# A SwiGLU feed-forward kernel: the first loads all issued from SyncE's queue instead of from SyncE and ScalarE

## The chip, the core and the metric

The kernel runs on one core of a Trainium2 chip. A core has five engines that run side by side and meet only at semaphores: TensorE (PE, matrix products; PEld is its weight load, which overlaps the products), VectorE (DVE), ScalarE (ACT), GpSimd (POOL) and SyncE (SP). A transfer (DMA) is issued by an instruction on SP's or ACT's own stream of instructions; the profile names these issues SPq and ACTq, and the packets that follow from them move on queue q1 (issued by SP) and queue q10 (issued by ACT). Both queues are served by the same 16 DMA engines.

The metric is device time in microseconds (us) of one execution. Before the change it is 163.66 us, the median of three runs from 163.46 to 163.86.

## The reference

The kernel computes a gated feed-forward layer: x is 2048 rows of 640, the gate and up weights are 640 x 1536, the down weight is 1536 x 640, all bfloat16.

```python
def reference(x, w_gate, w_up, w_down):
    g = _silu(x @ w_gate)
    u = x @ w_up
    return (g * u) @ w_down
```

## The kernel before, in words

The rows of x are taken in four blocks of 512 (NSB = 4, S_BLK = 512). For each block the hidden dimension of 1536 is walked in 12 column groups of 128 (KF = 12). For a group, five matmuls over the 640 input columns (KD = 5) make `pg` (gate) and five make `pu` (up); `proj` at L193 writes both, so line L195 carries them. ScalarE takes silu of `pg` (L212), VectorE multiplies it with `pu` (L213) and leaves the result in `aT`. After the 12 groups the block is projected down (L270 for the last 128 columns, L299 for the first 512) and stored. VectorE also works out the last four rows of x with dot products (L148) beside all this, and that has no part in the change.

The matmuls need x turned, with its columns on the partitions (`xT`), while it lies in memory row by row. For the first 256 rows TensorE turns it: `load_x` brings two chunks of 128 rows into `x_sb` (L86), `transpose_chunk` turns each with five matmuls against an identity (L186), and ScalarE and VectorE copy the results into `xT` (L191). All other rows are turned by a crossbar load: `turn_x` (L108 to L110) issues a DMA that transposes on its way. The first crossbar load brings rows 256 to 511 (called here *the first turn*).

The weights come in chunks of column groups, W_CHUNKS = (0,2), (2,4), (4,8), (8,12). The first chunk, 256 columns of gate and of up, is wanted first; it was cut at K_CUT = 2 into a part with input groups 0 and 1 and a part with input groups 2 to 4.

What this document calls the head of the kernel are the first nine or so microseconds:

- SP issues x chunk 0 (L112), gate groups 0:2, up groups 2:5, and the first turn (L121). ACT issues x chunk 1 (L113), gate groups 2:5, up groups 0:2. The loop at L115 to L120 crosses them over in this way. Only then does ACT run a one-column activation (L122), whose use is that the table for silu is loaded early.
- SP goes on with the second weight chunk (gate, up), the third, the fourth, the down weight (L126), the turn of the next 512 rows, and so on. All of these are issued from SP (L123 to L141), so each stands in SP's stream behind the ones before it.
- TensorE follows the order written in `head()` (L217 to L251), fixed by `keep_order`: 18 small matmuls on a tile of ones that produce nothing used (L177, `warm`), the five transposes of x chunk 0, the five of chunk 1, two more of the small ones, then 14 matmuls on gate for the first 256 rows (L237), 10 on up for the same rows (L195), and then, for rows 256 to 511, five on gate and five on up for each of two column groups. The last kind needs the first turn. After it the loop over the groups of 512 columns begins.

Completion semaphores of the DMAs are taken in rotation from a set of eight; an issue waits for the completion of the DMA that used the same semaphore before, eight DMAs earlier in the program.

Of the kernel before, what the change touches and what calls it, by code (L numbers as in the profile page):

```python
# [10 lines left out]
def _body(  # L11
# [8 lines left out]
    nc = tc.nc  # L20
# [12 lines left out]
    KD = D // P  # L33
# [10 lines left out]
    K_CUT = 2  # L44
    ROW_J = 0
    W_CHUNKS = [(0, 2), (2, 4), (4, 8), (8, 12)]
# [12 lines left out]
    wg_sb = consts.tile([P, KD, F], bf16)  # L59
    wu_sb = consts.tile([P, KD, F], bf16)  # L60
# [14 lines left out]
    wg_v = w_gate.rearrange("(kd p) f -> p kd f", p=P)  # L75
    wu_v = w_up.rearrange("(kd p) f -> p kd f", p=P)
    wd_v = w_down.rearrange("(kf p) d -> p kf d", p=P)

    def wslice(a, b):
        return slice(a * P, b * P)  # L80

    def load_w(eng, dst, src, a, b):
        eng.dma_start(out=dst[:, :, wslice(a, b)], in_=src[:, :, wslice(a, b)])

    def load_x(eng, c0, c1):
        eng.dma_start(out=x_sb[:, c0:c1, :], in_=x_v[:, c0:c1, :])  # L86
# [21 lines left out]
    def turn_x(c0, c1):  # L108
        s_sl = slice(c0 * P, c1 * P)
        nc.sync.dma_start_transpose(out=xT[:, :, s_sl], in_=xt_v[s_sl])  # L110

    load_x(nc.sync, 0, 1)  # L112
    load_x(nc.scalar, 1, 2)  # L113
    f_sl = wslice(*W_CHUNKS[0])
    for dst, src, first, second in (  # L115
        (wg_sb, wg_v, nc.sync, nc.scalar),
        (wu_sb, wu_v, nc.scalar, nc.sync),
    ):
        for eng, k_sl in ((first, slice(0, K_CUT)), (second, slice(K_CUT, KD))):
            eng.dma_start(out=dst[:, k_sl, f_sl], in_=src[:, k_sl, f_sl])  # L120
    turn_x(PE_X, SUB)  # L121
    nc.scalar.activation(silu_first[:], ones[:, 0:1], ACT.Silu)  # L122
    for a, b in W_CHUNKS[1:]:  # L123
# [6 lines left out]
    def turn_w(dst, src):  # L130
# [7 lines left out]
        out=x_row[:],  # L138
        in_=x2[S - T : S, :].rearrange("t d -> (t d)").partition_broadcast(P),
# [114 lines left out]
    for sb in range(NSB):  # L254
# [27 lines left out]
        for q in range(P // Q):  # L282
            nc.scalar.dma_start(
                out=out2[
                    sb * S_BLK : sb * S_BLK + n_t, DA + q * Q : DA + (q + 1) * Q
                ].rearrange("(i r) c -> r i c", r=Q),
                in_=ot_q[q * Q : (q + 1) * Q, :].rearrange("r (i c) -> r i c", c=Q),
            )

        for j in range(SUB):  # L290
# [5 lines left out]
            for c0, c1, tag in cols:  # L296
# [10 lines left out]
                if c1 < D:  # L307
                    nc.scalar.copy(ot[:], po[:])  # L308
                    eng = nc.sync
                else:  # L310
                    nc.vector.tensor_copy(out=ot[:], in_=po[:])  # L311
                    eng = nc.scalar
# [81 lines left out]
def kernel(tc, *args):  # L394
    _body(tc, *args)
    tc.close()
    tc.compile()
    _trim(tc.nc)
# [30 lines left out]
```

## Time and profile before

| what | value |
|---|---|
| runs, median (lowest to highest) | 163.66 us (163.46 to 163.86) |
| span of the profiled execution, first to last instruction | 162.2 us |
| around the span (median less span) | 1.46 us |
| VectorE busy | 110.9 us, 68% of the span |
| ScalarE busy | 42.7 us, 26% |
| TensorE weight loads busy | 77.9 us, 48% |
| DMA moved | 15.86 MB, 98 GB/s over the span |
| share of the 16 DMA engines, queue of SP and queue of ACT | 37.7% and 4.1% |

The page is of one execution. The span runs from the first to the last instruction of the core; the runs' times hold about 1.5 us more than it. A busy TensorE in the profile is a TensorE with matmuls in its pipe; how fast they follow each other has to be read from their starts. For DMAs there are three views: when the issuing engine spent time on the issue, how long after the start of the issue the transfer had landed (its semaphore complete), and how many packets of which size moved in a stretch of time on each queue. The loads of weights move in packets of 512 B (first and second chunk) or 1024 B, those of x chunks in packets of 1280 B, and crossbar loads in packets under 512 B, so they can be told apart.

### The profile page before, as it was taken

The numbers are of one execution on the slowest core, as the hardware profiler recorded it, in microseconds if no ns is written. First come the engines' busy times: TensorE is split into PE (matmuls) and PEld (weight loads), VectorE is DVE, ScalarE is ACT, GpSimd is POOL, SyncE is SP. The second block draws the span as 40 slices with busy tenths as digits, with TensorE's granted clock in tenths as the row PEclk, the third lists the DMA queues.
The fourth block names the chain that finished last, engine by engine and source line by source line (L and its number), as shares of the span: only waits on it lengthen the run. The fifth ranks groups of instructions, "written<-read, shape, count | busy, mean of one in ns | idle before, by whom it ended". The sixth has DMA issues, their size and how long they took to land.

```text
span 162.2 us, 2118 instructions
## 1 busy us (share of the span) xinstructions
PE 159.8 (99%) x798; PEld 77.9 (48%) x798; DVE 110.9 (68%) x249; ACT 42.7 (26%) x74; POOL 0.6 (0%) x6
## 2 busy tenths in 40 slices
PE   9999999999999999999999999999999999999995
PEld 8854444444444444444444444444444444445454
DVE  2042233599469999979919999979964999993000
ACT  5132222112222222221222322221214222222121
POOL 1000000000000000000000000000000000000000
PEclk9999999999999999999999999999999999999999
DMA  7999999994179992003110000000320000000312
GB/s 208 258 339 348 362 218 249 219 234 94 34 185 178 224 195 61 4 0 34 65 65 0 0 4 2 0 0 2 63 69 32 0 0 0 0 0 4 50 39 73
DMA packets 42441, 15.86 MB, mean 98 GB/s; under 512 B 33216, under 2 KB 42304, under 8 KB 42432
## 3 DMA queue, kind: packets, MB, share of 16 engines
q1 hardware_dynamic: 33536, 14.72, 37.7%
q10 hardware_dynamic: 8896, 1.02, 4.1%
q8 instruction: 6, 0.10, 0.2%
q14 instruction: 3, 0.02, 0.1%
HBM read 6.88 MB, written 2.62 MB: 59 GB/s over the span
## 4 chain that ended last, share of the span: by engine, by line
PE 99%; DVE 0%; issue 0%
PE pu L195 32%; PE pg L195 31%; PE po_a L299 26%; PE po_t L270 6%; PE pw L177 1%; PE pg L237 1%; PE pt L186 1%; DVE ot_b L311 0%; DVE ones L106 0%
## 5 line engine op out<-in xcount | busy, mean ns | idle before, releaser
L195 PE MATMUL pu<-xT,wu_sb 128*128 128x512 bf16 (+2 forms) x250 | 59.8, 370 | 0.0
L195 PE MATMUL pg<-xT,wg_sb 128*128 128x512 bf16 (+2 forms) x240 | 58.5, 374 | 0.0
L213 DVE TENSOR_TENSOR aT<-sg,pu 128x512 bf16<-128x512 f32 (+1 forms) x48 | 32.8, 683 | 32.8 <-PE pu L195 28.1
L212 ACT ACTIVATE sg<-pg 128x512 f32<-128x512 f32 (+1 forms) x48 | 28.6, 596 | 71.2 <-PE pg L195 68.1
L299 PE MATMUL po_a<-wd_sb,aT 128*128 128x512 bf16 (+2 forms) x216 | 42.8, 358 | 0.0
L148 DVE SCALAR_TENSOR_TENSOR prod<-wgT,x_row 128x640 f32<-128x640 bf16 x48 | 39.4, 821 | 1.1
L148 DVE SCALAR_TENSOR_TENSOR prod<-wuT,x_row 128x640 f32<-128x640 bf16 x48 | 39.4, 822 | 1.0
L195 PEld LDWEIGHTS <-wu_sb 128*128 128x128 bf16 x250 | 24.4, 98 | 27.6 <-DMA wu_sb<-in_w_up_dram 0.3
L195 PEld LDWEIGHTS <-wg_sb 128*128 128x128 bf16 x240 | 23.5, 98 | 26.9
L299 PEld LDWEIGHTS <-aT 128*128 128x128 bf16 x216 | 20.7, 98 | 21.6
L308 ACT CAST ot<-po_a 128x512 bf16<-128x512 f32 (+1 forms) x17 | 9.5, 560 | 32.0 <-PE po_a L299 20.8
L270 PE MATMUL po_t<-aT,wd_sb 128*128 128x512 bf16 (+1 forms) x48 | 10.4, 366 | 0.0
L270 PEld LDWEIGHTS <-wd_sb 128*128 128x128 bf16 x48 | 4.7, 98 | 5.1
L311 DVE CAST ot_b<-po_a 128x128 bf16<-128x128 f32 x1 | 0.3, 291 | 9.9 <-PE po_a L299 9.9
L279 ACT CAST ot_t<-po_t 128x512 bf16<-128x512 f32 (+1 forms) x4 | 2.2, 558 | 11.6 <-PE po_t L270 11.6
L148 DVE DVE_READ_ACCUMULATOR prod<-wuT,x_row 128x1 f32 x48 | 3.9, 82 | 0.0
L148 DVE DVE_READ_ACCUMULATOR prod<-wgT,x_row 128x1 f32 x48 | 3.9, 82 | 0.0
L281 DVE STREAM_TRANSPOSE ot_q<-ot_t 128x512 bf16<-128x512 bf16 (+1 forms) x4 | 2.7, 678 | 1.7 <-ACT ot_t L279 1.7
L177 PE MATMUL pw<-ones 128*128 128x128 bf16 x20 | 2.5, 313 | 0.4 <-DVE ones L106 0.4
L191 DVE COPY xT<-pt 128x384 bf16<-128x384 bf16 x2 | 0.7, 358 | 2.9 <-PE pt L186 2.9
L237 PE MATMUL pg<-xT,wg_sb 128*128 128x128 bf16 (+1 forms) x14 | 2.3, 360 | 0.0
L177 PEld LDWEIGHTS <-ones 128*128 128x128 bf16 x20 | 2.1, 148 | 0.4 <-DVE ones L106 0.4
(15 smaller groups left out, 7.6 us busy)
## 6 DMA issues: line engine op xcount, KB each, us to landing
wd_sb<-in_w_down_dram SPq DMA_DIRECT2D x1, 1920.0 KB, 14.5
out_dram<-ot SPq DMA_DIRECT2D x15, 128.0 KB, 1.7
wg_sb<-in_w_gate_dram SPq DMA_DIRECT2D x2, 640.0 KB, 7.7
wu_sb<-in_w_up_dram SPq DMA_DIRECT2D x2, 640.0 KB, 8.7
x_row<-in_x_dram SPq DMA_DIRECT2D x1, 640.0 KB, 4.7
out_dram<-ot_q ACTq DMA_DIRECT2D x12, 32.0 KB, 1.9
wg_sb<-in_w_gate_dram SPq DMA_DIRECT2D x1, 320.0 KB, 4.9
wu_sb<-in_w_up_dram SPq DMA_DIRECT2D x1, 320.0 KB, 5.4
```

What stands on the lines that cost most here:

```text
L148: nc.vector.scalar_tensor_tensor(out=prod[:], in0=wT[:, fc, :], scalar=1.0, in1=x_row[:, t, :], op0=ALU.mult, op1=ALU.mult, accum_out=acc[ ...
L177: nc.tensor.matmul(pw[:, 0:P], lhsT=ones[:], rhs=ones[:], start=True, stop=True)
L186: nc.tensor.transpose(out=pt[:, kd - k0, :], in_=x_sb[:, c, kd * P : (kd + 1) * P], identity=ident[:],)
L195: nc.tensor.matmul(ps[:, c0:c1], lhsT=w_sb[:, kd, fc * P : (fc + 1) * P], rhs=xT[:, kd, sb * S_BLK + c0 : sb * S_BLK + c1], start=(kd == 0 ...
L212: nc.scalar.activation(sg[:, 0:n_s], pg[:, 0:n_s], ACT.Silu)
L213: nc.vector.tensor_tensor(out=aT[:, fc, s0 : s0 + n_s], in0=sg[:, 0:n_s], in1=pu[:, 0:n_s], op=ALU.mult)
L237: nc.tensor.matmul(pg[:, c0:c1], lhsT=wg_sb[:, kd, wslice(fc, fc + 1)], rhs=xT[:, kd, c0:c1], start=(kd == 0 and c0 == 0), stop=(kd == KD ...
L270: nc.tensor.matmul(po_t[:], lhsT=wd_sb[:, kf, DA:D], rhs=aT[:, kf, sb * S_BLK : sb * S_BLK + n_t], start=(kf == 0), stop=(kf == KF - 1),)
L279: nc.scalar.copy(ot_t[:], po_t[:])
L281: nc.vector.transpose(out=ot_q[:], in_=ot_t[:])
L299: nc.tensor.matmul(po[:], lhsT=aT[:, kf, s0 : s0 + P], rhs=wd_sb[:, kf, c0:c1], start=(kf == 0), stop=(kf == KF - 1),)
L308: nc.scalar.copy(ot[:], po[:])
```

## The change

All loads of the head are issued by SP, one after another: x chunk 0, x chunk 1, gate groups 0:2, gate groups 2:5, the whole of up's first chunk in one DMA, then the first turn. ScalarE issues none of them; its first work is the activation with its table load. Everything after that stands in the same order as before. One DMA fewer is issued in all, since up's first chunk is no longer cut.

```diff
     load_x(nc.sync, 0, 1)
-    load_x(nc.scalar, 1, 2)
+    load_x(nc.sync, 1, 2)
     f_sl = wslice(*W_CHUNKS[0])
-    for dst, src, first, second in (
-        (wg_sb, wg_v, nc.sync, nc.scalar),
-        (wu_sb, wu_v, nc.scalar, nc.sync),
-    ):
-        for eng, k_sl in ((first, slice(0, K_CUT)), (second, slice(K_CUT, KD))):
-            eng.dma_start(out=dst[:, k_sl, f_sl], in_=src[:, k_sl, f_sl])
+    for k_sl in (slice(0, K_CUT), slice(K_CUT, KD)):
+        nc.sync.dma_start(out=wg_sb[:, k_sl, f_sl], in_=wg_v[:, k_sl, f_sl])
+    load_w(nc.sync, wu_sb, wu_v, *W_CHUNKS[0])
     turn_x(PE_X, SUB)
     nc.scalar.activation(silu_first[:], ones[:, 0:1], ACT.Silu)
     for a, b in W_CHUNKS[1:]:
```

## The prediction

> **What bounds the kernel now.** I read the page first: busy times and the chain that ended last.
>
> ```profile
> span 162.2 us, 2118 instructions
> ...
> PE 159.8 (99%) x798; PEld 77.9 (48%) x798; DVE 110.9 (68%) x249; ACT 42.7 (26%) x74; POOL 0.6 (0%) x6
> ...
> PE 99%; DVE 0%; issue 0%
> ```
>
> TensorE is the whole chain. A load costs time only where it makes TensorE wait, and each such wait in the head moves the end by as much. So I read the timeline of the head next (start, duration, engine; the bracket is an idle time and what ended it).
>
> ```profile
> 0.00 0.40 SPq L86 DMA_DIRECT2D x_sb<-in_x_dram  x1
> 0.12 0.41 ACTq L86 DMA_DIRECT2D x_sb<-in_x_dram  x1
> ...
> 0.57 0.45 ACTq L120 DMA_DIRECT2D wg_sb<-in_w_gate_dram  x1
> ...
> 1.04 0.51 ACTq L120 DMA_DIRECT2D wu_sb<-in_w_up_dram  x1
> 1.43 1.63 SPq L110 DMA_TRANSPOSE xT<-in_x_dram  x1
> ...
> 3.61 2.34 PE L237 MATMUL pg<-xT,wg_sb 128*128 128x128 bf16 x14
> ...
> 5.80 1.01 PEld L195 LDWEIGHTS <-wu_sb 128*128 128x128 bf16 x10 [0.32 <-DMA wu_sb<-in_w_up_dram]
> 5.80 1.29 PE L195 MATMUL pu<-xT,wu_sb 128*128 128x256 bf16 x10
> ...
> 6.92 0.71 PE L195 MATMUL pg<-xT,wg_sb 128*128 128x256 bf16 x5
> ```
>
> Issue plus time to landing gives when each load is there; the start of its first reader gives when it is wanted.
>
> - x chunk 1: 0.12 + 2.7 = 2.82; its weight loads come after the five transposes of chunk 0, which start at 2.29 and follow every 0.11: 2.83. No slack.
> - gate 0:2: 0.46 + 2.8 = 3.26, wanted 3.51. Gate 2:5: 0.57 + 3.6 = 4.17, wanted 4.47.
> - up 2:5: 0.92 + 4.7 = 5.62. Up 0:2: 1.04 + 4.7 = 5.74. The last gate matmul starts at 5.53 and its five predecessors of that size, from 4.47, came every 0.212, so up is wanted at 5.74 and used at 5.80: a wait of 0.06.
> - first turn: 1.43 + 5.4 = 6.83. The ten up matmuls from 5.80 follow every 0.11, as those after them do, and end at 6.90; gate goes on at 6.92. Slack 0.07.
> - second chunk: gate 3.11 + 4.9 = 8.01, wanted 9.00; up 3.73 + 5.4 = 9.13, wanted 9.97. Later loads have more: the third gate chunk 5.32 + 5.6 = 10.9, wanted near 13.2.
>
> The same 256-column matmul takes 0.212 up to 5.7 and 0.11 from 5.8. TensorE runs at half pace for its first 5.4 us of work, so in this stretch it is late itself, and loads have only to keep up with that.
>
> **The change: what SP now does.** SP takes over x chunk 1 (0.41) and gate 2:5 (0.45); up as one DMA has the size and shape of the second chunk's gate load (0.57) in place of 0.47; each added issue brings a gap of some 0.05. New issue times: x chunk 1 0.46, gate 0:2 0.92, gate 2:5 1.38, up 1.88, first turn 2.50, second chunk 4.18 and 4.80. So x chunk 1 is issued 0.34 later, the first turn and all behind it 1.07 later.
>
> *Upper bound*: every landing moves with its issue. Then x chunk 1 lands at 3.16, gate 2:5 at 4.98, up at 6.58, the first turn at 7.90. From up TensorE would be at the turn's reader at 6.58 + 1.10 = 7.68, so the turn binds: 7.90 - 6.88 = 1.02 us. The second chunk, at 9.08 and 10.2, is wanted at 10.0 and 11.0 by then. Price 1.02.
>
> *Lower bound*: landings are set by the bytes ahead, not by the issue. The packet views speak for this one. Packets and the share of each queue, 0.9 to 1.1, 1.3 to 1.5, 2.5 to 2.75 and 5 to 5.25 us:
>
> ```profile
> DMA packets 8, 0.01 MB, mean 51 GB/s; under 512 B 0, under 2 KB 8, under 8 KB 8
> ```
>
> ```profile
> DMA packets 31, 0.04 MB, mean 192 GB/s; under 512 B 1, under 2 KB 31, under 8 KB 31
> ...
> q10 hardware_dynamic: 1, 0.00, 1.7%
> ```
>
> ```profile
> DMA packets 130, 0.06 MB, mean 248 GB/s; under 512 B 9, under 2 KB 130, under 8 KB 130
> ```
>
> ```profile
> DMA packets 42, 0.01 MB, mean 46 GB/s; under 512 B 37, under 2 KB 42, under 8 KB 42
> ```
>
> A first packet moves about 1.0 us after its issue (SP's x chunk, issued at 0.00). ACT's x chunk, issued at 0.12, has its first packet only in 1.3 to 1.5, behind SP's chunk: the second queue buys no place. Issued at 0.46 it could begin at 1.46, the same time within 0.06. For the others I add up the bytes: 255 kB have moved by 2.0, 416 by 2.5, 543 by 3.0, 684 by 3.5, 826 by 4.0, 984 by 4.5. In the new order gate 2:5 begins after 459 kB, near 2.67 (its issue allows 2.38); up after 656 kB, near 3.4 (allows 2.88); the turn after 984 kB, at 4.5 (allows 3.50, and 5.1 for its last part by the 1.63 us its issue takes). Each is ready before its turn in the stream. SP's queue alone also keeps the rate: 291 to 294 GB/s at 7.0 to 8.5 us in 512 B packets, against 248 to 316 for the two queues between 2.5 and 4.5. I therefore take landings as unchanged, with 0.06 for x chunk 1 (bounds 0 and 0.33).
>
> *The turn.* Its packets (under 512 B) begin at 4.0, 122 by 4.5 and 367 more by 5.0, nearly stop from 5.0 to 5.25, and run at 566 in the half microsecond from 5.5. In the stop only a few last 512 B packets move. The same is seen at 22.3 to 22.9, where 6 and 7 packets of the down weight move per 0.3 us and the next turn starts only after them. I read it so: a crossbar load advances when the slowest DMA engine is through with the loads ahead. Those loads are the same bytes after the change, so the turn lands at 6.83, up to 0.15 later if fewer of its packets went ahead of the stop.
>
> *Up.* ACT's queue moved its last 512 B packets at 5.0 to 5.25 (2) and 31 at 4.5 to 4.75, yet up 0:2 had landed only at 5.74; the two x chunks landed 1.2 and 1.4 us after their first packets. With up wholly ahead of the turn on one queue I expect it by 5.6, so the wait of 0.06 goes. The Trainium skill, "DMA: Bandwidth & Descriptors", section on queues, rings and completion order, says the semaphore write of a DMA lands only after every earlier write of that DMA engine, across its queues. By that rule up 0:2's completion on ACT's queue was held behind turn packets of SP's queue, and the change would free it: a gain, but no more than the 0.06 that TensorE waited; the trace agrees in the lateness, and cannot show the order itself.
>
> *ScalarE.* Its table load begins at 1.58 and lasts 1.28, to 2.86; without three issues it begins near 0.2 and is done by 1.5. Its first needed work, the copy at 2.99, waits for TensorE's transposes. Gain nothing; loss nothing. POOL issues no load. SP's later issues: up's second chunk was already held at its issue (1.55 us instead of 0.57, until 5.28), which takes up the later start at 4.80, so the queue refills at the same time.
>
> **Sum.** x chunk 1 +0.06, so gate ends at 5.80; up is there; ten matmuls at 0.11 end at 6.90; the turn, between 6.83 and 6.98, is used between 6.92 and 7.00 instead of 6.92: 0 to 0.08, taken as +0.05. Span 162.2 + 0.05, with the 1.46 us around it 163.7 us. All after 7 us keeps its slack.
>
> **Rivals.**
>
> *The delay is carried* (slower). SP becomes the bound: descriptors of one issuer come too slowly, and x chunk 1, gate and the turn move with their issues. For it: the slack of x chunk 1 and of the turn is 0.01 and 0.07, and between 2.5 and 2.75 the rate sags to 248 GB/s, as if descriptors were short even with two issuers. Against it: the sums above, with 0.3 to 1.0 us to spare for all but x chunk 1. It decides from a turn landing 0.4 late; price up to 1.02, 164.7; half carried 164.2.
>
> *The pace of TensorE rises later* (slower). Half pace lasted from 0.40 to 5.80. If a gap for x chunk 1 at 2.83 made that stretch start again, full pace would come 5.4 later, at 8.2; 2.4 us at half pace lose 1.2: 164.9. Against it: the gap would be 0.06 to 0.33 us. The Trainium skill, "TensorE: Matmul & The Clock Gate", part 1, says full clock comes after a busy window of about 3.4 us that runs freely. By that rule a missed window would be an estimated 3.4 us more at half pace, some 1.7 us of loss, 165.4; the trace shows one step of pace near 5.8, which neither supports nor refutes the window's length.
>
> *Loads land earlier and TensorE can use it* (faster). If full pace comes earlier in other runs, up at 5.74 and the turn at 6.83 bound them; without the stop, the turn's 1280 packets at 566 per 0.5 us need 1.13 from 4.5, landing near 6.3. At most some 0.5 of this is used: 163.2. Against it: in this profile TensorE itself is at the turn only at 6.88.
>
> **Chances.** Forecast (within 0.2%, which is 0.33 us and about what a measurement of this kernel tells from no change) 0.56, its own range 163.4 to 164.0. Delay carried 0.30, pace later 0.04, together slower 0.34. Earlier loads 0.10. The range is 163.25 to 164.6: it leaves out half of the faster case, the late pace, and the last tenth of the carried delay.
>
> **What would show it.** Right: x chunk 1 landing at 2.8 to 2.95, no idle before the up matmuls, the second part of gate at 6.9 to 7.0, first small packets near 4.2 and a stop near 5. Wrong: an idle TensorE before 2.9 or before 6.9 of over 0.3 us, DMA engines idle between 1.5 and 4.5, or 256-column matmuls at 0.212 beyond 6.

## The result, and the profile after

| | before | after |
|---|---|---|
| median of 12 runs each (lowest to highest) | 163.58 us (163.14 to 163.86) | 163.97 us (163.49 to 164.50) |
| ratio after to before, 95% interval | | 1.0030 (1.0018 to 1.0042) |
| span of the profiled execution | 162.2 us | 162.3 us |

The change costs 0.39 us, 0.24% by the medians and 0.30% by the ratio. The profiled execution of the changed kernel took 163.67 us, near the lowest of its twelve; a second profile of it, told below, has a span of 162.8 us. The ratios in this document leave out executions that took over 1.5% longer than the fastest of their kernel, and the one profile of e10 below is of such an execution (212 us, granted clock 0.756), so that only its DMA rows are read. (All line numbers after L119 are smaller by three in the changed kernel: L195 is L192, L237 is L234.)

The page after, busy times and the chain that ended last:

```profile
span 162.3 us, 2117 instructions
...
PE 159.8 (98%) x798; PEld 77.6 (48%) x798; DVE 111.0 (68%) x249; ACT 42.9 (26%) x74; POOL 0.6 (0%) x6
...
PE 96%; DMA 2%; SPq 1%; DVE 0%; issue 0%
PE pu L192 32%; PE pg L192 31%; PE po_a L296 26%; PE po_t L267 6%; DMA wg_sb<-in_w_gate_dram 2%; PE pg L234 1%; SPq L86 1%; SPq L116 0%; DVE ot_b L308 0%
```

Before, the chain was TensorE from beginning to end. Now it runs through SP's issues of x (L86) and gate (L116), then a DMA into `wg_sb` for 2% of the span, and only then into TensorE: the page ties the end of the kernel to the landing of a gate load. The timeline of the head shows which (start, duration, engine):

```profile
0.00 0.87 SPq L86 DMA_DIRECT2D x_sb<-in_x_dram  x2
0.12 1.28 ACT L119 ACT_TABLE_LOAD   x1
...
0.91 0.95 SPq L116 DMA_DIRECT2D wg_sb<-in_w_gate_dram  x2
...
1.90 0.49 SPq L83 DMA_DIRECT2D wu_sb<-in_w_up_dram  x1
...
2.43 2.12 SPq L110 DMA_TRANSPOSE xT<-in_x_dram  x1
...
4.94 1.06 PE L234 MATMUL pg<-xT,wg_sb 128*128 128x256 bf16 x6 [0.20 <-DMA wg_sb<-in_w_gate_dram]
...
5.91 1.27 PE L192 MATMUL pu<-xT,wu_sb 128*128 128x256 bf16 x10
...
7.11 0.70 PE L192 MATMUL pg<-xT,wg_sb 128*128 128x256 bf16 x5
```

The 256-column gate matmuls, the readers of gate 2:5, start at 4.94 instead of 4.47, after an idle TensorE; the matmuls that need the first turn start at 7.11 instead of 6.92.

The idle time before gate is not the last wait of the head, though. The ten up matmuls start 0.05 us after up has landed (5.86); at 0.11 each they are through near 7.01, and the turn's readers start 0.04 after the turn has landed (7.07). Had gate been on time, TensorE would still have waited for up and for the turn. From there to the end the two profiles keep their distance: the loop over groups of 512 columns begins at 9.29 instead of 9.11, and the spans differ by as much, 0.18 us.

Behind all three late landings is a thin stream. The DMA view for 2.5 to 3.0 us, first before, then after:

```profile
DMA packets 261, 0.13 MB, mean 254 GB/s; under 512 B 13, under 2 KB 261, under 8 KB 261
```

```profile
DMA packets 139, 0.07 MB, mean 135 GB/s; under 512 B 7, under 2 KB 139, under 8 KB 139
...
q1 hardware_dynamic: 139, 0.07, 51.0%
```

The 16 engines are busy half of the time although, of the 0.98 MB of the five plain loads of the head (those ahead of the turn), only 0.37 MB had moved by 2.5. The loads land as follows (us from the span's start; landing records of the trace; the second profile of each kernel is from the runs r1 and r2 below):

| landed | x 0 | x 1 | gate 0:2 | gate 2:5 | up, last part | first turn | MB moved by 4 us |
|---|---|---|---|---|---|---|---|
| before | 2.25 | 2.85 | 3.25 | 4.20 | 5.75 | 6.82 | 0.83 |
| before, r1 | 2.46 | 2.85 | 3.44 | 4.32 | 5.56 | 6.54 | 0.87 |
| after | 2.31 | 2.81 | 3.67 | 4.90 | 5.86 | 7.07 | 0.65 |
| after, r2 | 2.29 | 2.78 | 3.26 | 5.07 | 6.06 | 7.28 | 0.65 |

Both x chunks are on time. From gate 2:5 on everything is late: by 0.6 to 0.9 us itself, by 0.1 to 0.5 for up, by 0.25 to 0.75 for the turn. Gate 0:2 was late in the first profile alone, where its reader started at 3.71 instead of 3.61.

### The profile page after: what moved, and what is told of

Its sections match the earlier page's. It is cut to its first block, busy times and chain, and to the rows that moved or that the text cites. A ratio compares the mean times of both kernels' runs of the same rounds, so it can differ in the third digit from the quotient of the medians.

```text
span 162.3 us, 2117 instructions
## 1 busy us (share of the span) xinstructions
PE 159.8 (98%) x798; PEld 77.6 (48%) x798; DVE 111.0 (68%) x249; ACT 42.9 (26%) x74; POOL 0.6 (0%) x6
## 4 chain that ended last, share of the span: by engine, by line
PE 96%; DMA 2%; SPq 1%; DVE 0%; issue 0%
PE pu L192 32%; PE pg L192 31%; PE po_a L296 26%; PE po_t L267 6%; DMA wg_sb<-in_w_gate_dram 2%; PE pg L234 1%; SPq L86 1%; SPq L116 0%; DVE ot_b L308 0%
## 5 line engine op out<-in xcount | busy, mean ns | idle before, releaser
L192 PE MATMUL pu<-xT,wu_sb 128*128 128x512 bf16 (+2 forms) x250 | 59.7, 370 | 0.0
L192 PE MATMUL pg<-xT,wg_sb 128*128 128x512 bf16 (+2 forms) x240 | 58.5, 374 | 0.0
L192 PEld LDWEIGHTS <-wu_sb 128*128 128x128 bf16 x250 | 24.4, 98 | 27.4 <-DMA wu_sb<-in_w_up_dram 0.2
L192 PEld LDWEIGHTS <-wg_sb 128*128 128x128 bf16 x240 | 23.5, 98 | 27.1
L234 PE MATMUL pg<-xT,wg_sb 128*128 128x128 bf16 (+1 forms) x14 | 2.1, 318 | 0.2 <-DMA wg_sb<-in_w_gate_dram 0.2
```

The source lines that it names most:

```text
L192: nc.tensor.matmul(ps[:, c0:c1], lhsT=w_sb[:, kd, fc * P : (fc + 1) * P], rhs=xT[:, kd, sb * S_BLK + c0 : sb * S_BLK + c1], start=(kd == 0 ...
L234: nc.tensor.matmul(pg[:, c0:c1], lhsT=wg_sb[:, kd, wslice(fc, fc + 1)], rhs=xT[:, kd, c0:c1], start=(kd == 0 and c0 == 0), stop=(kd == KD ...
```

## The experiments

The question was what makes SP's stream of loads thin out between 2.5 and 4.0 us. The theories, by the letters of the expectations: **S**, a load lands a fixed time after its issue, so a late issue is a late landing; **T**, the price is the late issue of the first turn; **Q**, one queue alone moves less than two, whenever its loads are issued; **X**, the long issue of the crossbar load slows the queue's loads ahead of it; and **S2**, formed after e1 to e8, that a load issued when data already flows comes out slowly at first, on either queue, so that what counts is how early the last loads of the head are issued. The experiments ran on three chips; each ratio is against the kernel before on the same chip (163.3 to 163.6 us).

| run | ratio (95% interval) | issue of the last load of the first chunks, us | GB/s in 2.5-3, 3-3.5, 3.5-4 us | MB by 4 us |
|---|---|---|---|---|
| before | | 1.04 | 254, 282, 284 | 0.83 |
| r1, before again | 1.0003 (0.9988 to 1.0018) | 1.04 | 302, 320, 328 | 0.87 |
| e3, only up's part changed | 1.0005 (0.9991 to 1.0020) | 0.92 | 323, 319, 292 | 0.83 |
| e9, one queue, three issues | 1.0072 (1.0046 to 1.0098) | 1.00 | 278, 323, 302 | 0.78 |
| after | 1.0030 (1.0018 to 1.0042) | 1.90 | 135, 201, 224 | 0.65 |
| r2, after again | 1.0031 (1.0015 to 1.0047) | 1.89 | 176, 196, 152 | 0.65 |
| e2, x chunk 1 back on ACT | 1.0050 (1.0031 to 1.0069) | 1.42 | 269, 138, 136 | 0.64 |
| e1, gate 2:5 back on ACT | 1.0061 (1.0039 to 1.0083) | 1.39 | 366, 221, 133 | 0.72 |
| e4, SP's issues late | 1.0062 (1.0033 to 1.0090) | 1.89 | 338, 264, 121 | 0.71 |
| e7, turn moved away | 1.0233 (1.0180 to 1.0285) | 1.89 | 194, 216, 215 | 0.68 |
| e10, both queues held | 1.0075 (1.0039 to 1.0111) | 1.77 | 104, 165, 291 | 0.61 |
| e6, gate 2:5 on ACT at 0.38 | 1.0121 (1.0095 to 1.0147) | 1.46 | 365, 323, 198 | 0.77 |
| e5, the same, with a small load | 1.0125 (1.0099 to 1.0150) | 1.97 | 371, 282, 115 | 0.71 |
| e8, gate 2:5 on ACT at 1.28 | 1.0134 (1.0104 to 1.0164) | 1.39 | 204, 85, 203 | 0.62 |

One thing beside the loads moves these times: TensorE's pace. Each execution begins at half pace (256-column matmuls every 0.213 us, later every 0.11), and the pace rises at different times: near 3.3 us in r2, by 4.0 in e2, e3 and e7, near 5.4 in the first profile after, 5.8 before, 6.6 in r1, and only between 8.4 and 9.2 in the profiles of e1, e5, e6 and e9. e9 shows what that does:

```profile
6.73 2.34 PE L189 MATMUL pu<-xT,wu_sb 128*128 128x256 bf16 x10
8.86 0.85 PE L189 MATMUL pg<-xT,wg_sb 128*128 128x256 bf16 x5
```

The ten up matmuls take 2.34 us there, against 1.27 in the changed kernel, and the readers of the turn start at 8.86 although the turn landed at 6.80. In e1, e5 and e6 the turn had likewise landed 1.1 to 1.55 us before its readers started. So the ratios of these four hold a loss by the pace as well as a wait for loads, and do not measure late loads alone. In all four, TensorE had stood idle for 0.37 to 0.75 us just before or between the transposes, at 3.2 to 3.8 us; whether that holds the pace back was not tried by itself. Nor is one profile the median: the profile of e1 is of its longest execution (165.63, median 164.27), and the twelve executions of e4 fall into seven from 163.65 to 164.20 and five from 165.12 to 165.70, its profile being of one at 163.84.

**Parts undone, four runs.** e1, on the changed kernel:

```diff
-    for k_sl in (slice(0, K_CUT), slice(K_CUT, KD)):
-        nc.sync.dma_start(out=wg_sb[:, k_sl, f_sl], in_=wg_v[:, k_sl, f_sl])
+    for eng, k_sl in ((nc.sync, slice(0, K_CUT)), (nc.scalar, slice(K_CUT, KD))):
+        eng.dma_start(out=wg_sb[:, k_sl, f_sl], in_=wg_v[:, k_sl, f_sl])
```

> The changed kernel with one part undone: gate groups 2:5 of the first chunk are issued by ScalarE again, as its first instruction (near 0.12 us instead of SP's 1.4). Theory S (a load lands with its issue, because one issuer hands out descriptors too slowly, and the late gate 2:5, 4.90 in the changed kernel, is the price): gate 2:5 lands by 4.2, TensorE does not stop before the 256-column gate matmuls, ratio 0.999 to 1.001; but x chunk 1 now has gate bytes beside it and may land up to 0.3 later than 2.8, which would cost as much. Theory T (the price is the first turn, which SP issues late): the turn is issued near 1.95 instead of 2.43, about half of the shift, and the ratio is about 1.0015. Theory Q (one queue drains slower than two): two queues are in use, ratio 1.000.

Measured: gate 2:5 landed early, at 3.23, but x chunk 1 only at 3.69 (TensorE stood 0.37 us for it), gate 0:2 at 4.67, up at 6.17, the turn at 7.47: ratio 1.0061, no better than the whole change. ScalarE's gate load, issued at 0.12, goes ahead of SP's x chunk 1, issued at 0.46. And the turn, issued half a microsecond earlier than in the changed kernel (1.90 for 2.43), landed 0.2 to 0.4 later than in the two profiles of the changed kernel: against T.

e2, on the changed kernel:

```diff
-    load_x(nc.sync, 1, 2)
+    load_x(nc.scalar, 1, 2)
```

> The changed kernel with another part undone: x chunk 1 is issued by ScalarE again (near 0.12 us), all else stays on SP, so gate 0:2, gate 2:5, up and the turn are each issued about 0.46 earlier than in the changed kernel. Theory S: gate 0:2 lands at 3.25, gate 2:5 near 0.92 + 3.5 = 4.4, about when it is wanted: ratio 1.000 to 1.001. Theory T: turn issued near 1.95, half of the loss, 1.0015. Theory Q: all 512 B loads are on one queue still, the rate sags between 2.3 and 4 us as in the changed kernel (under 200 GB/s from 2.5 to 2.75), gate 2:5 lands at 4.7 or later, ratio 1.002 to 1.003.

Measured: gate 2:5, issued 0.48 earlier than in the changed kernel, landed at 5.37 instead of 4.90 to 5.07; ratio 1.0050. Of the matmul lines of the timeline,

```profile
5.41 0.83 PE L234 MATMUL pg<-xT,wg_sb 128*128 128x256 bf16 x6 [0.86 <-DMA wg_sb<-in_w_gate_dram]
6.45 1.26 PE L192 MATMUL pu<-xT,wu_sb 128*128 128x256 bf16 x10 [0.21 <-DMA wu_sb<-in_w_up_dram]
```

TensorE stands 0.86 us for gate and 0.21 for up. S in its simple form falls, T as well (turn issued at 1.95, landed at 7.68). Q had asked for a thin stream, and it was there, only later (138 and 136 GB/s from 3.0).

e3, on the kernel before:

```diff
-    for dst, src, first, second in (
-        (wg_sb, wg_v, nc.sync, nc.scalar),
-        (wu_sb, wu_v, nc.scalar, nc.sync),
-    ):
-...
+    for eng, k_sl in ((nc.sync, slice(0, K_CUT)), (nc.scalar, slice(K_CUT, KD))):
+        eng.dma_start(out=wg_sb[:, k_sl, f_sl], in_=wg_v[:, k_sl, f_sl])
+    load_w(nc.sync, wu_sb, wu_v, *W_CHUNKS[0])
```

> The kernel before with only up's part of the change: the first chunk of up goes whole on SP, x chunk 1 and gate 2:5 stay on ScalarE. Theory S: x and gate land as before (2.85, 3.25, 4.2), up lands by 5.6 since no completion waits on the other queue, the turn is issued 0.1 later: ratio 0.998 to 1.000. Theory T: ratio 1.000 (the turn's issue moves 0.1). Theory Q: the second half of the head is on one queue, up lands at 5.9, ratio 1.001.

Measured: up landed at 5.39, the turn at 6.62, ratio 1.0005. Joining up's two parts on SP costs nothing that a comparison can tell. SP's queue moved nearly all of the 292 GB/s in 3.5 to 4.0 us here, the first sign against Q.

e4, on e3 (`small_load` loads 128 rows of 64 B):

```diff
     load_x(nc.sync, 0, 1)
+    small_load(0)
     load_x(nc.scalar, 1, 2)
...
+    small_load(1)
     load_w(nc.sync, wu_sb, wu_v, *W_CHUNKS[0])
```

> As e3, with two small loads (8 KB each, 128 rows of 64 B, read by nobody) put on SP where x chunk 1 and gate 2:5 stand in the changed kernel: SP's issue times of gate 0:2, up, the turn and all later loads are then those of the changed kernel, while x chunk 1 and gate 2:5 come early from ScalarE. Two loads more than e3, nothing left out. Theory S: gate 0:2 lands near 3.7 as in the changed kernel (TensorE waits some 0.1 to 0.2), gate 2:5 by 4.3, up by 5.8: ratio 1.000 to 1.0015, clearly less than the change. Theory T: the turn lands as late as in the changed kernel, near 7.05, ratio 1.003. Theory Q: 1.000.

Measured: ratio 1.0062, where no theory had over 1.003. The turn landed at 7.17, near T's 7.05, but the longest wait is earlier: gate 0:2, now issued at 0.91 behind ScalarE's gate 2:5 (0.55), came after it, and TensorE stood 0.63 us until 4.86 for it. The run mixes order and delay and separates nothing by itself.

**Repeats.** The same two kernels again, on one chip.

> The kernel before, unchanged, run against itself, for what a comparison can tell and for a second profile on the chip of the other runs. All theories: ratio 1.000, its interval shows the resolution. For the reading of the others it matters where x chunk 0 lands: 2.25 in the first profile of the kernel before, 2.7 in the three experiments that issue a load from ScalarE at 0.12; if it lands at 2.7 here too, the two queues delay the first chunk and the single queue wins back some 0.4 us there.

> The changed kernel, unchanged, on the same chip as the other runs. Expected: ratio 1.003 as before (1.002 to 1.004), x chunk 0 landed by 2.3, gate 2:5 near 4.9, DMA rate under 230 GB/s in 2.5 to 4.0 us.

Measured: 1.0003 (0.9988 to 1.0018) and 1.0031 (1.0015 to 1.0047). So the cost is real, and on this chip x chunk 0 landed at 2.46 before and 2.29 after: a gain of at most 0.2 there. The second profile of the changed kernel shows the wait for gate at its full length:

```profile
3.46 0.65 PE L234 MATMUL pg<-xT,wg_sb 128*128 128x128 bf16 x8
5.11 0.83 PE L234 MATMUL pg<-xT,wg_sb 128*128 128x256 bf16 x6 [1.00 <-DMA wg_sb<-in_w_gate_dram]
6.10 1.27 PE L192 MATMUL pu<-xT,wu_sb 128*128 128x256 bf16 x10 [0.16 <-DMA wu_sb<-in_w_up_dram]
7.32 0.71 PE L192 MATMUL pg<-xT,wg_sb 128*128 128x256 bf16 x5
```

Here the small gate matmuls already run at the full pace (eight in 0.65 us with their pipe; 1.03 in the first profile), so TensorE was ready early and stood 1.00 us for gate 2:5. Again it is not the last wait: up landed at 6.06 and the turn at 7.28, and their readers started 0.04 after each. In r1 TensorE was never idle but kept half pace until 6.6, and its readers of the turn started at 7.33. The span of r2 is 0.2 us longer than that of r1 by a later load:

```profile
15.09 0.76 PEld L192 LDWEIGHTS <-wu_sb 128*128 128x128 bf16 x5 [0.53 <-DMA wu_sb<-in_w_up_dram]
15.10 1.25 PE L192 MATMUL pu<-xT,wu_sb 128*128 128x512 bf16 x5
```

That is the third chunk of up, issued at 6.61 and landed at 15.05 (5.66 and 12.66 in r1). TensorE's matmuls were within 0.02 us of r1's from the readers of the turn until then, and are 0.2 later from here on. In the first profile of the changed kernel this chunk landed at 13.96 and held nothing.

**The same load on the other queue, three tries.** e5 and e6 were to issue gate 2:5 from ScalarE at about the time at which SP issues it in the changed kernel, by putting it behind the activation with its table load; e5 has one small load in its old place on SP, e6 none:

```diff
+    nc.scalar.activation(silu_first[:], ones[:, 0:1], ACT.Silu)
     load_x(nc.sync, 0, 1)
     load_x(nc.sync, 1, 2)
...
-        nc.sync.dma_start(out=wg_sb[:, k_sl, f_sl], in_=wg_v[:, k_sl, f_sl])
+    nc.scalar.dma_start(out=wg_sb[:, k_b, f_sl], in_=wg_v[:, k_b, f_sl])
+    nc.sync.dma_start(out=small[:], in_=x_v[:, 0, 0:32])
     load_w(nc.sync, wu_sb, wu_v, *W_CHUNKS[0])
```

> The changed kernel with gate 2:5 issued by ScalarE behind its table load and activation, so near 1.65 us, which is 0.27 later than SP issues it in the changed kernel; in its place on SP stands a small load (128 rows of 64 B, read by nobody), so all of SP's other issues keep their times. Only the queue of gate 2:5 differs, not its time. Theory S (a load lands with its issue): gate 2:5 lands at 1.65 + 3.5 = 5.15, ratio 1.004 or more. Theory Q (one issuer's queue hands out its 512 B packets too slowly before 4 us, a second queue adds to it, whatever the issue times): the rate in 2.5 to 4.0 us is over 250 GB/s, gate 2:5 lands by 4.6, ratio at most 1.0015. Theory T (the turn's late issue is the price): the turn stays late, 1.003.

> As e5 without the small load: up is issued near 1.38 and the turn near 1.9 on SP, gate 2:5 near 1.65 on ScalarE, x chunk 1 after x chunk 0 on SP. Theory Q: as e5 or better, ratio 0.999 to 1.001, unless up, issued first, holds gate 2:5 back by some 0.3. Theory S: gate 2:5 lands at 5.15, ratio 1.003. Theory T: half of the turn's delay, 1.0015.

Measured: 1.0125 and 1.0121. Neither did what it was built for. ScalarE's timeline in e5:

```profile
0.12 1.28 ACT L113 ACT_TABLE_LOAD   x1
0.38 0.48 ACTq L119 DMA_DIRECT2D wg_sb<-in_w_gate_dram  x1
1.41 0.20 ACT L113 ACTIVATE silu_first<-ones 128x1 f32<-128x1 bf16 x1
```

The DMA is issued at 0.38 while the table is still loading and before the activation that stands ahead of it in the program: work on the engine does not hold the issue. Gate was issued 0.08 before SP's x chunk 1: in e5 ScalarE's queue had moved 108 packets by 2.0 us, of the 384 of gate, and x chunk 1 came out beside the rest. It landed at 3.71 and 3.75 instead of 2.8, and TensorE stood 0.69 and 0.71 us for it. With that the pace rose late, as told above. The two show what a wrong order costs here, and nothing of S or Q.

e8 holds the issue by a real dependency (on the changed kernel):

```diff
+    nc.gpsimd.memset(wg_sb[:, K_CUT:KD, 0 : 2 * P], 0.0)
     load_x(nc.sync, 0, 1)
...
-        nc.sync.dma_start(out=wg_sb[:, k_sl, f_sl], in_=wg_v[:, k_sl, f_sl])
+    nc.scalar.dma_start(out=wg_sb[:, k_b, f_sl], in_=wg_v[:, k_b, f_sl])
```

> The changed kernel with gate 2:5 on ScalarE's queue, held back until GpSimd has written zeros over the place that it loads (the load overwrites them, so the result is unchanged): it is issued near 1.3 us, behind SP's gate 0:2 and close to the 1.38 at which SP issues it in the changed kernel. e5 and e6 were meant to do this but ScalarE issued at 0.38, ahead of x chunk 1. Theory Q (a second queue supplies more, whatever the time of the issue): over 270 GB/s in 2.5 to 4.0 us, gate 2:5 lands by 4.5 although its issue is no earlier, up by 5.5, ratio 0.998 to 1.001. Theory S (it is the later issue): gate 2:5 lands near 4.9, ratio 1.002 to 1.003. Theory X: up and turn are issued 0.5 earlier, the rate stays low, gate 2:5 lands by 4.6, up near 5.9.

Measured: gate 2:5 issued at 1.28 and landed at 6.09, ratio 1.0134. From 3.0 to 3.5 us:

```profile
DMA packets 83, 0.04 MB, mean 85 GB/s; under 512 B 0, under 2 KB 83, under 8 KB 83
...
q10 hardware_dynamic: 74, 0.04, 40.9%
q1 hardware_dynamic: 9, 0.00, 3.9%
```

ScalarE's gate load (1.28) and SP's up (1.39) have both been issued 1.6 us ago and more, on two queues, and hardly anything moves. This is against Q, against S, which had 4.9, and against X, which had 4.6.

**The crossbar load taken away.** e7 issues the first turn behind the second weight chunk:

```diff
-    turn_x(PE_X, SUB)
     nc.scalar.activation(silu_first[:], ones[:, 0:1], ACT.Silu)
     for a, b in W_CHUNKS[1:]:
         load_w(nc.sync, wg_sb, wg_v, a, b)
         load_w(nc.sync, wu_sb, wu_v, a, b)
+        if a == 2:
+            turn_x(PE_X, SUB)
```

> The changed kernel with the first turn moved behind the second weight chunk on SP (order x, x, gate 0:2, gate 2:5, up, gate chunk 2, up chunk 2, turn). It is not meant to be fast: the turn lands some 1.5 us later and TensorE waits for it (ratio 1.006 to 1.012). What it tells: whether the slow stretch of SP's queue (135 to 225 GB/s between 2.5 and 4.0 us in the changed kernel) comes from the crossbar load's issue behind it. Theory Q (one queue alone supplies 512 B packets too slowly this early): the rate in 2.5 to 4.0 us stays under 230 GB/s and gate 2:5 lands near 4.9. Theory X (the crossbar load's issue slows the queue's descriptors ahead of it): the rate is over 270 GB/s, gate 2:5 lands by 4.4 and up by 5.4.

Measured: 194 to 216 GB/s from 2.5 to 4.0 us and gate 2:5 at 4.91, as in the changed kernel, with the turn's issue moved from 2.43 to 3.56. X falls. (TensorE stood 2.01 us for the turn; the ratio 1.0233 is larger than expected.)

**Issue time against number of queues.** The last two runs set S2 against Q with opposite outcomes. e9 has one queue and early issues:

```diff
-    load_x(nc.sync, 0, 1)
-    load_x(nc.sync, 1, 2)
-...
-        nc.sync.dma_start(out=wg_sb[:, k_sl, f_sl], in_=wg_v[:, k_sl, f_sl])
+    load_x(nc.sync, 0, PE_X)
+    load_w(nc.sync, wg_sb, wg_v, *W_CHUNKS[0])
     load_w(nc.sync, wu_sb, wu_v, *W_CHUNKS[0])
```

> The changed kernel, still one queue, with three issues instead of five ahead of the turn: both x chunks in one DMA (0.00), the first gate chunk whole (near 0.46), up whole (near 1.0), turn near 1.5. Same bytes, the same 512 B and 1280 B rows, all issued by about 1.0 us, as in the kernel before and in e3, where 0.83 to 0.87 MB had moved by 4 us against 0.65 in the changed kernel. Theory S2 (what counts is how early the last loads are issued: a load issued after the data has begun to flow comes out slowly, on either queue): at least 0.80 MB by 4.0 us, gate lands whole by 4.3, up by 5.5. Theory Q (one queue alone is slow before 4 us): 0.70 MB or less by 4.0, gate near 4.9. Time: x now lands as a whole near 2.85, so TensorE starts its transposes some 0.5 later and gate 0:2 comes with 2:5; with S2 ratio 1.000 to 1.004, with Q 1.005 or more.

e10 has both queues as before and late issues:

```diff
+    nc.gpsimd.memset(wg_sb[:, 1:4, 0 : 2 * P], 0.0)
     load_x(nc.sync, 0, 1)
     load_x(nc.scalar, 1, 2)
```

> The kernel before with both queues as they are and the same order of loads, but gate's two parts, and with them all that stands behind on both queues, held until GpSimd has written zeros over part of their place (the loads overwrite them): the weights are issued near 1.28 and 1.75 on both engines, the turn near 2.2, about as late as in the changed kernel, with two queues. Theory S2: it is slow like the changed kernel, 0.75 MB or less by 4.0 us, gate 2:5 lands at 4.8 or later, ratio 1.003 or more. Theory Q (two queues supply enough whatever the time): over 270 GB/s from 2.6 us on, so 0.78 MB or more by 4.0, gate 2:5 lands by 4.6, ratio at most 1.002.

Measured, the same stretch of 2.5 to 3.0 us in the DMA view, first e9, then e10:

```profile
DMA packets 252, 0.14 MB, mean 278 GB/s; under 512 B 8, under 2 KB 252, under 8 KB 252
...
q1 hardware_dynamic: 252, 0.14, 89.9%
```

```profile
DMA packets 100, 0.05 MB, mean 104 GB/s; under 512 B 6, under 2 KB 100, under 8 KB 100
q1 hardware_dynamic: 70, 0.04, 27.0%
q10 hardware_dynamic: 30, 0.02, 10.8%
```

One queue, issued by 1.0 us, keeps the engines 90% busy here and at 302 to 323 GB/s up to 4.0. Two queues, issued between 1.28 and 1.77, leave them 38% busy. Q falls by the bytes: it asked for at most 0.70 MB by 4 us in e9 and for 0.78 or more in e10, and they moved 0.78 and 0.61. The times of e10 agree, with a ratio of 1.0075 where Q had at most 1.002, and so does e8, where late loads on two queues flow thinly too. S2 is met by e10 and missed a little by e9 (0.78 MB for 0.80, gate at 4.58 for 4.3, up at 5.59 for 5.5).

The time of e9, 1.0072, lies where Q had it (1.005 or more) and not where S2 had it (at most 1.004). In its profile, with both x chunks in one DMA, x landed at 3.20, TensorE stood 0.75 us for it and then kept half pace until about 9.1; the up matmuls and the readers of the turn waited for no load. e9 also has three loads ahead of the turn instead of five, so it doesn't tell early issues from few issues. That late issues are enough for a thin stream is shown by e8 and e10; that they are all that thins it in the changed kernel is not.

No version tried beats the kernel before; e3, with one DMA fewer, is its equal.

## Why the prediction was right and wrong

**The number.** 163.97 us lies inside the stated range, but not by the working: that gave +0.05 us, and the measured cost is 0.39. The range held it because it was drawn to take in most of the rival.

**The bound** was read rightly: TensorE sets the end, and what a load makes it wait is lost. **x chunk 1** was given 0 to 0.06 of delay, landing at 2.8 to 2.95; it landed at 2.81 and 2.78. **ScalarE's** table load moved to 0.12 and brought nothing. **The second chunk** kept its slack: gate landed at 8.28, wanted at 9.18. But "All after 7 us keeps its slack" failed in r2, where the third chunk of up cost 0.20.

**The step that failed** is "Each is ready before its turn in the stream", and with it "I therefore take landings as unchanged". It took a load as ready 1.0 us after its issue, the time of the first packet of x chunk 0. That is not yet a full stream, and the profile of before showed the difference: 51 GB/s at 0.9 to 1.1, 192 at 1.3 to 1.5, and over 340 only from 1.5 us on, 1.5 after the first issue. For loads issued later it was longer still: in e10 the weights, issued at 1.28, reached 291 GB/s at 3.5 to 4.0, 2.2 us after it; in the changed kernel the bytes of all loads ahead of up had moved by 4.0, when 331 GB/s were reached, 2.1 after up's issue at 1.90; in e1 and e2, with up issued at 1.39 and 1.42, 272 GB/s were reached only at 4.5, 3.1 after. With 2.1 instead of 1.0 the forecast's own sum turns over: gate 2:5 is due in the stream at 2.67 and full at 1.38 + 2.1 = 3.5, up is due at 3.4 and full at 4.0. (The 2.1 is taken from the runs that it is to explain, so this shows the size of the error and proves no rule.) The sag to 248 GB/s that the prediction named as a sign for the rival was no sure one: r1, with the same kernel, moved 302 GB/s from 2.5 to 3.0. The mis-sized terms are the landings taken as unchanged: gate 2:5 landed 0.70 later in the first profile (4.20 to 4.90), and TensorE stood idle for it by 0.20 there and by 1.00 in r2; up and the turn landed later too. The turn is the one that sets the time: its readers started at 7.11 and 7.32, where the sum had 6.92 to 7.00.

**The turn.** Forecast at 6.83 to 6.98, measured 7.07 and 7.28. The reading that it waits for the plain loads ahead and not for its issue held: in e1, e2, e3, e4, e9, the changed kernel and r2 it landed 1.2 to 1.35 us after up (e3: 5.39 and 6.62; e2: 6.41 and 7.68), while its issue moved from 1.43 to 2.43. Before and in r1, with up on two queues, it was 1.07 and 0.98. (Not all packets under 512 B are the turn's, as the prediction counted them: 9 move at 2.5 to 2.75, before it begins at 4.0. Its 122 by 4.5 us is a little high.) But "those loads are the same bytes" does not make them end at the same time; they ended later because the stream was thin.

**Up** was expected by 5.6, from completions no longer held behind the turn. In the changed kernel it landed at 5.86 and 6.06, the completions of all 16 DMA engines within 0.2 us. In e3, where the stream was full, it landed at 5.39 on one queue, against 5.75 and 5.56 on two, and the time did not change. So the gain of 0.06 had no weight either way.

**The rivals.** What happened is *the delay is carried*, in part: 0.39 of its 1.02 us, with its sign (thin stream, idle TensorE before gate and at the turn), though not by x chunk 1 and not with every landing moving by its issue (up: issued 0.9 later, landed 0.1 to 0.5 later). Its weight of 0.30 was too small beside the 0.56 for no change, whose own limit of 0.33 us the result passes by little. Of the signs of being wrong, the idle DMA engines were there in both profiles, the idle TensorE of over 0.3 us only in r2. *The pace rises later* was not seen in the changed kernel, whose 256-column matmuls ran at 0.11 from 5.91 at the latest. It was seen in e1, e5, e6 and e9, where the pace rose at 8.4 to 9.2: the prediction had 8.2, for a gap before x chunk 1, and a time of 164.9, and the profiled executions took 165.2 to 165.6. That TensorE's gap is the reason is not shown.

**What stays open.** Why the stream thins is not shown: loads issued from 1.28 us on needed 2 to 3 us to flow, and no view gives descriptors. Nor does S2 rank the versions by what they cost. In e2 every later load was issued 0.48 earlier than in the changed kernel, gate 2:5 already at 0.91, where up in e9, issued at 1.00, flowed at over 300 GB/s; yet gate 2:5 landed later than in the changed kernel, and the ratio was 1.0050. e8 lost far more. In e2 x chunk 0 also lands 0.4 later (2.74), beside x chunk 1 on the other queue; in e8 two queues take up late loads side by side. Whether that is why was not tried. The number of loads that are in flight together was not varied by itself either.

## What to carry to other kernels

Count a load at the head of a kernel as useful from the time at which its stream is full, 2 to 3 us after its issue here for the late ones, not from its first packet; here, moving issues from one engine to another put the last of them 0.9 us later, after the data had begun to flow, and cost 0.3%. The number of queues by itself did not decide: one queue kept a full stream in e9, and two did not in e8 and e10. The four runs that had issued the first chunks by 1.04 us (before, r1, e3, e9) kept a full stream; e2, with gate 2:5 at 0.91 and only up later, did not. Before reading a small difference between two profiles as the price of a load, see at what time TensorE's pace rose in each. And when a load is put on another queue, check which one is then issued first: in e5, 0.08 us of lead for gate made x chunk 1 land 0.9 us later.

## What the runs showed of the hardware that was not expected

A load on another queue that is issued a little earlier takes its place in the stream: in e1 ScalarE's 192 KB, issued at 0.12, landed at 3.23 and SP's x chunk 1, issued at 0.46, at 3.69; in e5, with issues at 0.38 and 0.46, the two moved side by side and x chunk 1 landed at 3.71 instead of 2.8. The Trainium skill, "DMA: Bandwidth & Descriptors", section "Issuing engines are not separate DMA queues", says that issuing from several engines saves only the time of the issue, which is usually small relative to the transfer. The first half fits e8, e9 and e10; of the second, the 0.3 to 1.0 us by which the change delays the issues was here worth 0.39 us of 164.

A DMA issue on ScalarE came before the end of a table load and before an activation that stand ahead of it in the program (0.38 against 1.41 in e5).

TensorE's pace changed at about 5.8 us in the profile of before and at 6.6 in r1, which is the same kernel, and at 5.4 and 3.3 in the two of the changed kernel. The Trainium skill, "TensorE: Matmul & The Clock Gate", part 1, says the window that decides it runs freely and the point varies by run, by 0.5 us either way. The profiles agree that it varies; the spread here is 2 us for the changed kernel and some 6 us over all runs. An early change does not help where loads are late: r2 had the early pace, and its readers of the turn started at 7.32, those of the first profile at 7.11.
